# Late modulation rows from DMA transposes and VectorE product-sums, and half of the row statistics on ScalarE, in an adaLN + linear attention + SwiGLU block

## The chip, the cores and the metric

One NeuronCore of a Trainium2 chip runs the whole kernel in one launch. The metric is the device time in microseconds (us), the median of several runs. Below, PE is TensorE, DVE is VectorE, ACT is ScalarE, POOL is GpSimd, and SP is the engine that issues most of the DMAs (SPq and ACTq are the DMA-issuing parts of SP and ACT).

## What is computed

Everything is bf16, with S = 2048 rows, D = 1024, F = 3584 and 32 heads of width 32.

```python
x = A_x
mod = (silu(c) @ w_mod).reshape(1, 6, 1, D)        # w_mod is 1024 x 6144
sa, ca, ga, sb, cb, gb = mod[:, 0] ... mod[:, 5]    # six rows of D numbers
h = layernorm(x) * (1 + ca) + sa
q, k, v = split(h @ wqkv);  pq, pk = phi(q), phi(k) # phi(t) = (t+1 if t>0 else exp(t)) + 1e-6
o = (pq @ (pk^T v)) / (pq . sum(pk) + 1e-6)         # per head
x = x + ga * (o @ wo)
h = layernorm(x) * (1 + cb) + sb
out = x + gb * ((silu(h @ w_gate) * (h @ w_up)) @ w_down)
```

The rows `sa` and `ca` are needed at once; `ga`, `sb`, `cb`, `gb` are "late": each is silu(c), a vector of 1024, times a 1024 x 1024 slice of `w_mod`.

## The kernel before

The rows of x are cut into 16 tiles of 128 rows, and four tiles make a chunk of 512. Weights stay in a few large SBUF regions (M12, M3, M4, M5, M6, M7), of which views are used one after the other; `M4` holds the normalized, transposed and modulated activations of all four chunks.

**The order of work** is written out by hand. `add` appends a labelled step to `seq`; a label is (stage, chunk, number). `put` hangs further steps on a label, to be issued just after it. At the end a loop issues `seq` in order (lines 688 to 691). Every engine executes its own instructions in the order in which this loop issues them, and an instruction that waits holds up what stands behind it on its engine. The steps, in order: V,0 (eight groups); then for each chunk sc the stages KV,sc and, interleaved, Q,0 (only after chunk 0), K,sc+1 (eight groups) and V,sc+1 (eight groups); then Q,1 to Q,3 with the attention output; then GU,0 to GU,3 (28 steps of gate and up for each chunk); and D (down projection).

A **group** is eight matmuls of 128x512 into one PSUM bank. `nextbank` (line 237) hands out banks 0 to 4 in turn, so a group can begin when the group five before it has been taken out of its bank. For K and Q the bank is emptied by `phi_to` (line 242): one exp on ACT (L244), then two instructions on DVE (L245, L246). For V it is emptied by one copy on ACT (L267).

**Row statistics and normalization of a tile** (`ln`, line 223): DVE computes the statistics (`ln_stats`, L203 to L207), POOL computes the inverse deviation and shift (L209, L211) and the normalized tile (L218, 128x1024), and SP issues a DMA transpose into M4 (L227). Later `modulate` (L231, on DVE) applies 1+ca and sa. For chunk sc+1 these steps hang on K,sc,1 / 3 / 5 / 7 and V,sc,4 / 6 (lines 601 to 604).

**The late rows** come in blocks of 512 columns (`load_late`, 1 MB each, L299). Three ways lead from a block to the numbers: `late_vec` (L328) does `cb` on PE, 32 matmuls with one column each for a block; `late_sum` (L305, L307) does `ga`, `sb`, `gb` on DVE, eight instructions of 128x512 for a block that multiply by silu(c) per partition and add up in fp32, leaving a sum over partitions to be done; `late_split` (L312, L313) cuts this sum into a high and a low bf16 part, and PE sums over the partitions, with `late_cols` (L320, 8 matmuls with one column for a block) for `sb` and `late_bc` (L342, two 128x512 matmuls for a block, then a copy by ACT, L343) for `ga` and `gb`, which are wanted on all partitions. `ga` multiplies `wo` (L637) at K,3,2 to V,3,1 and `gb` multiplies `w_down` (L683) in GU,1, both on DVE.

Of the kernel before, what the change touches and what calls it, by code (L numbers as in the profile page):

```python
# [8 lines left out]
ACT = mybir.ActivationFunctionType  # L9
# [12 lines left out]
def kernel(  # L22
# [64 lines left out]
    def view(region, off, shape, dtype=BF16):  # L87
        n = 1
        for s_ in shape:
            n *= s_  # L90
        w = n * (2 if dtype == F32 else 1)
        ap = region[:, off:off + w]
        if dtype == F32:
            ap = ap.bitcast(F32)
        if len(shape) == 2:
            ap = ap.rearrange("p (a b) -> p a b", a=shape[0])
        elif len(shape) == 3:
            ap = ap.rearrange("p (a b c) -> p a b c", a=shape[0], b=shape[1])
        return ap
# [5 lines left out]
    wd_lo = view(M12, 14336, [14, D])  # L105
    wme = view(M3, 0, [DC, 2 * D])
    pqT = view(M3, 0, [NSC, HG, SCW])
    wml = [view(M3, 4096 * (1 + i), [DC, NB]) for i in range(3)]
    wd_hi = view(M3, 0, [14, D])
    pk = view(M5, 0, [STC, D])  # L110
    v_c = view(M5, 4096, [STC, HG, VW])
# [9 lines left out]
    accA = view(M5, 8256, [D], F32)  # L121
    hlA = [view(M5, 10304 + 1024 * i, [2, NB]) for i in range(2)]
    accG = view(M3, 12288, [D], F32)
    hlG = view(M3, 14336, [2, NB])
# [14 lines left out]
    def load_x(st):  # L139
        nc.sync.dma_start(out=xs[st % 6], in_=x2[st * P:(st + 1) * P, :])  # L140
# [43 lines left out]
    ones = const.tile([P, P], BF16, name="ones")  # L184
    nc.gpsimd.memset(ones[:], 1.0)
    scF = const.tile([P, DC], F32, name="scF")

    scT = const.tile([P, DC], BF16, name="scT")
    nc.scalar.activation(out=scT[:], in_=c_sb[:], func=ACT.Silu)
    nc.scalar.copy(out=scF[:], in_=scT[:])  # L190

    def warm(n):
        for _ in range(n):
# [5 lines left out]
    def ln_stats(st):  # L199
# [12 lines left out]
                                op0=ALU.mult, op1=ALU.mult)  # L212
        stat[st] = (rstd, nmr)

    def ln_xn(st, pool):
        rstd, nmr = stat.pop(st)
        if pool:
            nc.gpsimd.tensor_scalar(out=xns[st % 6], in0=xs[st % 6], scalar1=rstd[:], scalar2=nmr[:],  # L218
                                    op0=ALU.mult, op1=ALU.add)
# [81 lines left out]
    def late_sum(acc, kb, slot, js):  # L301
        dst = acc[:, kb * NB:(kb + 1) * NB]
        for j in js:
            if j == 0:
                nc.vector.tensor_scalar_mul(out=dst, in0=wml[slot][:, 0, :], scalar1=scF[:, 0:1])  # L305
            else:
                nc.vector.scalar_tensor_tensor(out=dst, in0=wml[slot][:, j, :], scalar=scF[:, j:j + 1], in1=dst,  # L307
                                         op0=ALU.mult, op1=ALU.add)

    def late_split(acc, kb, hl):  # L310
        src = acc[:, kb * NB:(kb + 1) * NB]
        nc.vector.tensor_copy(out=hl[:, 0, :], in_=src)  # L312
        nc.vector.tensor_tensor(out=hl[:, 1, :], in0=src, in1=hl[:, 0, :], op=ALU.subtract)  # L313

    def late_cols(q, kb, hl):
        o = 320 + 8 * q
        for ii in range(NB // P):
            col = o + kb * (NB // P) + ii
            for s_ in range(2):
                nc.tensor.matmul(bank[7][:, col:col + 1], lhsT=hl[:, s_, ii * P:(ii + 1) * P], rhs=ones[:, 0:1],  # L320
                                 start=False, stop=(s_ == 1), skip_group_check=True)

    def late_vec(q, kb, slot):
        o = 320 + 8 * q
        for ii in range(NB // P):
            col = o + kb * (NB // P) + ii
            for j in range(DC):
                nc.tensor.matmul(bank[7][:, col:col + 1], lhsT=wml[slot][:, j, ii * P:(ii + 1) * P],  # L328
                                 rhs=scT[:, j:j + 1], start=False, stop=(j == DC - 1), skip_group_check=True)

    def late_fin(q):
        mps = bank[7][:, 320 + 8 * q:328 + 8 * q]
        if q == SB:
            nc.vector.tensor_copy(out=sbT[:], in_=mps)
        else:
            nc.vector.tensor_copy(out=m1[:, q, :], in_=mps)
            nc.vector.tensor_scalar_add(out=cb1T[:], in0=m1[:, q, :], scalar1=1.0)

    def late_bc(kb, hl, dst):
        b = nextbank()  # L340
        for s_ in range(2):
            nc.tensor.matmul(b[:], lhsT=ones[:], rhs=hl[:, s_, :], start=(s_ == 0), stop=(s_ == 1))  # L342
        nc.scalar.copy(out=dst[:, kb * NB:(kb + 1) * NB], in_=b[:])  # L343


    def tr0(st):
# [101 lines left out]
    def put(label, *fns):  # L448
        after.setdefault(label, []).extend(fns)
# [159 lines left out]
    def sums(acc, kb, slot, labels):  # L609
        for i, lab in enumerate(labels):  # L610
            put(lab, lambda i=i: late_sum(acc, kb, slot, (2 * i, 2 * i + 1)))
# [4 lines left out]
    put(("V", 1, 7), lambda: late_fin(CB))  # L616
    sums(accA, 0, 2, [("V", 1, k) for k in range(4)])
    put(("V", 1, 3), lambda: late_split(accA, 0, hlA[0]), lambda: load_late(SB, 1, 2))
    put(("K", 2, 2), lambda: late_bc(0, hlA[0], ga_bc))
    put(("K", 2, 3), lambda: nc.sync.dma_start(out=wo, in_=wo_v))  # L620
    sums(accA, 1, 0, [("V", 2, k) for k in range(4)])
    put(("V", 2, 3), lambda: late_split(accA, 1, hlA[1]))
    put(("K", 3, 0), lambda: late_bc(1, hlA[1], ga_bc))
    for kb in range(2):
        sums(accA, kb, 1 + kb, [("V", 3, 4 * kb + k) for k in range(4)])
    put(("V", 3, 4), lambda: late_split(accA, 0, hlA[0]))
    put(("KV", 3, 0), lambda: late_split(accA, 1, hlA[1]))
    put(("Q", 1, 2), lambda: late_cols(SB, 0, hlA[0]), lambda: late_cols(SB, 1, hlA[1]), lambda: late_fin(SB))
    put(("GU", 0, 18), lambda: load_late(GB, 0, 0), lambda: load_late(GB, 1, 1))
    gb_at = [("GU", 0, f) for f in range(21, FC)] + [("GU", 1, f) for f in range(8)]  # L630
    for kb in range(2):
        sums(accG, kb, kb, gb_at[5 * kb:5 * kb + 4])
        put(gb_at[5 * kb + 3], lambda kb=kb: late_split(accG, kb, hlG))
        put(gb_at[5 * kb + 5], lambda kb=kb: late_bc(kb, hlG, gb_bc))
# [88 lines left out]
```

## Time and profile before

| | |
|---|---|
| time, median of 3 runs | 842.72 us (842.72 to 843.25) |
| the profiled execution: its time / its span | 842.25 us / 840.4 us |
| granted TensorE clock | 0.999 |
| busy PE / DVE / ACT / POOL | 833.5 / 356.5 / 145.1 / 79.9 us |
| DMA | 128.62 MB, 153 GB/s in the mean |
| late rows: loads of `w_mod` | 8 of 1 MB |
| DMA transposes issued by SP / by ACT | 12 / 32 |

The span runs from the first to the last instruction; the execution's own time is 1.85 us longer. The profile gives, for each engine, when each instruction ran and what ended the idle time ahead of it; the chain of waits is followed back from the last instruction, at each step to what released it. V,0 begins at about 31 us of the span, K,1,0 at 60.7 us, K,2,0 at 90.7, K,3,0 at 120.6, Q,1,0 at 150.4, GU,0 at 210, GU,1 at 346 us.

### The profile page before, as it was taken

The page shows a single profiled execution, that of the slowest core. Times are in us where ns is not written, and L with a number is a line of the kernel's source. Part 1 is how long each engine was busy: PE and PEld are TensorE (multiplying, and loading weights), DVE is VectorE, ACT ScalarE, POOL GpSimd, SP SyncE. Part 2 cuts the span into 40 slices and gives each one's busy share as a digit, 9 for nine tenths or more (in the row PEclk, how much of TensorE's full clock was granted, in tenths as well). Part 3 has the DMA queues.
Part 4 walks back from the last instruction along what each step waited for, and adds up shares of the span by engine and source line. Part 5 has one row for each costly group of instructions (what it writes and reads, how often), then busy time and mean ns, then how long its engine had stood idle before and what let it go on. Part 6 is the DMA issues. An engine that isn't in the chain of part 4 may idle for free.

```text
span 840.4 us, 10723 instructions
## 1 busy us (share of the span) xinstructions
PE 833.5 (99%) x4292; PEld 391.3 (47%) x4292; DVE 356.5 (42%) x668; ACT 145.1 (17%) x271; POOL 79.9 (10%) x143
## 2 busy tenths in 40 slices
PE   8999999999999999999999999999999999999998
PEld 4454444544444444444444444444444444444445
DVE  5768779988655656635341111111101211111111
ACT  4333333323211111111110001111000111100000
POOL 2124220022122323100000000000000000000000
PEclk9999999999999999999999999999999999999999
DMA  9985491056599899787874225555322555211210
GB/s 291 310 244 138 133 243 46 16 154 133 126 225 225 224 226 287 190 248 226 251 241 142 76 69 151 151 151 152 105 75 82 156 155 152 76 38 44 76 69 26
DMA packets 203905, 128.62 MB, mean 153 GB/s; under 512 B 50768, under 2 KB 190032, under 8 KB 203856
## 3 DMA queue, kind: packets, MB, share of 16 engines
q1 hardware_dynamic: 163008, 98.58, 41.1%
q10 hardware_dynamic: 38544, 20.98, 11.4%
q0 software_dynamic: 2304, 8.39, 2.6%
q8 instruction: 33, 0.54, 0.3%
q14 instruction: 16, 0.13, 0.1%
HBM read 103.81 MB, written 12.58 MB: 139 GB/s over the span
## 4 chain that ended last, share of the span: by engine, by line
PE 97%; SPq 1%; DMA 1%; issue 0%; DVE 0%
PE bank L553 23%; PE bank L534 23%; PE bank L528 23%; PE bank L272 7%; PE bank L485 7%; PE bank L264 7%; PE bank L249 6%; DMA M<-in_w_mod_dram 1%; PE bank L458 1%; PE bank L281 1%; SPq L148 1%; SPq L145 0%; PE bank L342 0%; SPq L140 0%; PE bank L328 0%; PE bank L364 0%
## 5 line engine op out<-in xcount | busy, mean ns | idle before, releaser
L534 PE MATMUL bank<-M,M 128*128 128x512 bf16 x896 | 211.7, 379 | 0.0
L528 PE MATMUL bank<-M,M 128*128 128x512 bf16 x896 | 211.6, 379 | 0.0
L536 DVE TENSOR_TENSOR M<-bank,e 128x512 bf16<-128x512 f32 x112 | 77.5, 692 | 248.5 <-PE bank L534 247.1
L553 PE MATMUL bank<-M,M 128*128 128x512 bf16 (+2 forms) x728 | 148.0, 363 | 0.0
L531 ACT ACTIVATE e<-bank 128x512 f32<-128x512 f32 x112 | 66.8, 597 | 436.3 <-PE bank L528 423.6
L553 PEld LDWEIGHTS <-M 128*128 128x128 bf16 x952 | 90.9, 98 | 103.0
L534 PEld LDWEIGHTS <-M 128*128 128x128 bf16 x896 | 87.7, 98 | 105.7
L528 PEld LDWEIGHTS <-M 128*128 128x128 bf16 x896 | 87.3, 98 | 103.9
L556 DVE TENSOR_TENSOR M<-bank,M 128x512 bf16<-128x512 f32 (+2 forms) x34 | 22.5, 661 | 169.9 <-PE bank L553 169.9
L249 PE MATMUL bank<-M,M 128*128 128x512 bf16 x256 | 57.9, 379 | 1.0 <-DVE M L231 0.6
L485 PE MATMUL bank<-M,M 128*128 128x512 bf16 x256 | 57.9, 379 | 0.0
L272 PE MATMUL bank<-M,M 128*128 128x512 bf16 x256 | 57.7, 379 | 0.0
L264 PE MATMUL bank<-M,M 128*128 128x512 bf16 x256 | 55.9, 379 | 0.0
L244 ACT ACTIVATE e<-bank 128x512 f32<-128x512 f32 x64 | 37.8, 598 | 100.5 <-PE bank L272 48.8
L553 PE MATMUL bank<-M 128*128 128x512 bf16 x224 | 51.0, 379 | 0.0
L246 DVE SCALAR_TENSOR_TENSOR M<-bank,e 128x512 bf16<-128x512 f32 x64 | 44.3, 692 | 3.9
L264 PEld LDWEIGHTS <-M 128*128 128x128 bf16 x256 | 25.0, 98 | 30.2
L485 PEld LDWEIGHTS <-M 128*128 128x128 bf16 x256 | 25.0, 98 | 29.7
L249 PEld LDWEIGHTS <-M 128*128 128x128 bf16 x256 | 24.2, 98 | 29.5 <-DVE M L231 2.1
L245 DVE TENSOR_SCALAR e<-e 128x512 f32<-128x512 f32 x64 | 27.7, 433 | 23.4 <-ACT e L244 23.4
L272 PEld LDWEIGHTS <-M 128*128 128x128 bf16 x256 | 24.5, 98 | 27.6
L487 DVE TENSOR_TENSOR M<-bank,M 128x512 f32<-128x512 f32 x32 | 22.0, 689 | 13.3 <-PE bank L485 13.1
(74 smaller groups left out, 362.4 us busy)
## 6 DMA issues: line engine op xcount, KB each, us to landing
M<-in_B_w_gate_dram SPq DMA_DIRECT2D x56, 512.0 KB, 3.9
M<-in_B_w_up_dram SPq DMA_DIRECT2D x56, 512.0 KB, 4.9
M<-in_w_mod_dram SPq DMA_DIRECT2D x8, 1024.0 KB, 8.7
x_scratch<-M POOLq DMA_DIRECT2D x16, 512.0 KB, 5.6
M<-x_scratch ACTq DMA_DIRECT2D x16, 512.0 KB, 3.4
M<-in_B_w_down_dram SPq DMA_DIRECT2D x6, 1024.0 KB, 7.9
M<-in_A_x_dram SPq DMA_DIRECT2D x16, 256.0 KB, 6.6
M<-in_w_mod_dram SPq DMA_DIRECT2D x8, 512.0 KB, 7.1
```

Source lines behind the costliest of these rows:

```text
L244: nc.scalar.activation(out=e[:], in_=acc, func=ACT.Exp)
L245: nc.vector.tensor_scalar(out=e[:], in0=e[:], scalar1=1.0, scalar2=PHI_EPS, op0=ALU.min, op1=ALU.add)
L246: nc.vector.scalar_tensor_tensor(out=dst, in0=acc, scalar=0.0, in1=e[:], op0=ALU.max, op1=ALU.add)
L249: nc.tensor.matmul(acc[:], lhsT=M4[:, sc_, cc, t * P:(t + 1) * P], rhs=wk[:, cc, h * NB:(h + 1) * NB], start=(cc == 0), stop=(cc == DC - 1))
L264: nc.tensor.matmul(acc[:], lhsT=M4[:, sc_, cc, t * P:(t + 1) * P], rhs=wv[:, cc, h * NB:(h + 1) * NB], start=(cc == 0), stop=(cc == DC - 1))
L272: nc.tensor.matmul(acc[:], lhsT=wq[:, cc, qc * P:(qc + 1) * P], rhs=M4[:, sc_, cc, :], start=(cc == 0), stop=(cc == DC - 1))
L485: nc.tensor.matmul(acc[:], lhsT=oTs[st % 3][:, cc, :], rhs=wo[:, cc, hs], start=(cc == 0), stop=(cc == DC - 1))
L528: nc.tensor.matmul(g_ps[:], lhsT=wg_blk[:, cc, fs], rhs=M4[:, sc_, cc, :], start=(cc == 0), stop=(cc == DC - 1))
L531: nc.scalar.activation(out=sg[:], in_=g_ps[:], func=ACT.Silu)
L534: nc.tensor.matmul(u_ps[:], lhsT=wu_blk[:, cc, fs], rhs=M4[:, sc_, cc, :], start=(cc == 0), stop=(cc == DC - 1))
L536: nc.vector.tensor_tensor(out=gus[sc_][:, f, :], in0=u_ps[:], in1=sg[:], op=ALU.mult)
L553: nc.tensor.matmul(y_ps[:, 0:w], lhsT=gus[sc_][:, f, t * P:(t + 1) * P], rhs=wd(f)[:, c0:c1], start=(f == 0), stop=(f == FC - 1))
```

## The change

- **Late rows.** For each of `ga`, `cb`, `sb`, `gb` eight DMA transposes read `w_mod` from HBM straight into a transposed view `rowT` (the output column lies on the partitions). One DVE instruction for each block of 128 columns (`tensor_tensor_reduce`, 128x1024) multiplies with silu(c), spread over all partitions in `sc_bc`, and sums to one number per partition in `colF`; its elementwise products go to a scratch tile `prod`. `late_vec`, `late_split`, `late_cols` and the ones-matmuls are gone. Where a row is wanted on all partitions (`sc_bc`, `ga_bc`, `gb_bc`), DVE spreads the column over a 128x1024 tile (`spread`), PE transposes it in eight 128x128 pieces, and ACT copies 128x1024 out.
- **Places.** One transpose hangs on each step of Q,0 (`ga`), V,1 (`cb`), V,2 (`sb`) and GU,0,18 to 25 (`gb`); one product-sum on each step of V,1, V,2, V,3 and GU,1,0 to 7. `cb` uses the region of `wo`, so the load of `wo` is issued after the last product-sum of `cb`, at V,2,7 (before: at K,2,3); the multiplication of `wo` by `ga` starts at K,3,4 (before: K,3,2), that of `w_down` by `gb` at GU,1,10 (before: GU,1,7).
- **Row statistics.** Tiles 9, 11, 13, 15 (the odd ones of chunks 2 and 3) get their statistics on ACT: a Copy and a Square of 128x1024, both with an accumulated row sum; POOL turns these into mean, variance, inverse deviation and shift. The `ln` steps move to K,sc,0 / 1 / 3 / 4 and the modulations to V,sc,2 / 3. The load of x tiles 12 to 15 moves from V,1,7 to K,1,7.

```diff
+    rowT = [view(M3, 4096, [DC, DC, P]), view(M6, 0, [DC, DC, P])]
+    prod = [view(M5, 8256, [D], F32), view(M3, 12288, [D], F32)]
...
-    gb_bc = const.tile([P, D], BF16, name="gb_bc")
+    gb_bc = ga_bc
...
+    def ln_stats_act(st):
+        x_sb = xs[st % 6]
+        sm = small.tile([P, 2], F32, name="sm")
+        nc.scalar.activation(out=xns[st % 6], in_=x_sb, func=ACT.Copy, accum_out=sm[:, 0:1])
+        nmean = small.tile([P, 1], F32, name="nmean")
+        nc.gpsimd.tensor_scalar_mul(out=nmean[:], in0=sm[:, 0:1], scalar1=-1.0 / D)
+        nc.scalar.activation(out=xns[st % 6], in_=x_sb, func=ACT.Square, bias=nmean[:], accum_out=sm[:, 1:2])
+        veps = small.tile([P, 1], F32, name="veps")
+        nc.gpsimd.tensor_scalar(out=veps[:], in0=sm[:, 1:2], scalar1=1.0 / D, scalar2=LN_EPS,
+                                op0=ALU.mult, op1=ALU.add)
+        rstd = small.tile([P, 1], F32, name="rstd")
+        nc.gpsimd.tensor_tensor(out=rstd[:], in0=veps[:], in1=neg_half[:], op=ALU.pow)
+        nmr = small.tile([P, 1], F32, name="nmr")
+        nc.gpsimd.tensor_tensor(out=nmr[:], in0=nmean[:], in1=rstd[:], op=ALU.mult)
+        stat[st] = (rstd, nmr)
...
     def ln(st):
-        ln_stats(st)
+        if st >= 2 * STC and st % 2:
+            ln_stats_act(st)
+        else:
+            ln_stats(st)
         ln_xn(st, True)
         sc_, t = divmod(st, STC)
         nc.sync.dma_start_transpose(out=M4[:, sc_, :, t * P:(t + 1) * P], in_=xns[st % 6])
...
-    def load_late(q, kb, slot):
-        k0 = q * D + kb * NB
-        nc.sync.dma_start(out=wml[slot], in_=wm_v[:, :, k0:k0 + NB])
...
+    def load_late(q, i, js):
         for j in js:
+            nc.sync.dma_start_transpose(out=rowT[i][:, j], in_=wm_v[:, j, q * D:(q + 1) * D])
+
+    def late_sum(q, i, pr, bs):
+        for b in bs:
+            nc.vector.tensor_tensor_reduce(out=prod[pr].rearrange("p (j k) -> p j k", j=DC), in0=rowT[i][:, :, b, :],
+                                           in1=sc_bc[:].rearrange("p (j k) -> p j k", j=DC), scale=1.0, scalar=0.0,
+                                           op0=ALU.mult, op1=ALU.add, accum_out=colF[:, q, b:b + 1])
+
+    def late_fin(q):
+        if q == SB:
+            nc.vector.tensor_copy(out=sbT[:], in_=colF[:, q, :])
+        else:
+            nc.vector.tensor_copy(out=m1[:, q, :], in_=colF[:, q, :])
+            if q == CB:
+                nc.vector.tensor_scalar_add(out=cb1T[:], in0=m1[:, q, :], scalar1=1.0)
             else:
+                spread(nc.vector, m1[:, q, :])
+
+    def spread(eng, col):
+        eng.tensor_copy(out=rep[:], in_=col.unsqueeze(2).to_broadcast([P, DC, P]))
+
+    def late_bc(dst):
+        tp = nextbank()[:].bitcast(BF16).rearrange("p (c s) -> p c s", c=DC)
+        for cc in range(DC):
+            nc.tensor.transpose(tp[:, cc, :], rep[:, cc, :], ident[:])
+        nc.scalar.copy(out=dst[:].rearrange("p (c s) -> p c s", c=DC), in_=tp)
...
     for cc in range(6, 8):
         modulate(0, cc, saT, ca1T)
+    spread(nc.vector, scT[:])
     for cc in range(6):
...
     for sc in (2, 3):
-        put_ln(sc, [("K", sc - 1, 1), ("K", sc - 1, 3), ("K", sc - 1, 5), ("K", sc - 1, 7),
-                    ("V", sc - 1, 4), ("V", sc - 1, 6)])
+        put_ln(sc, [("K", sc - 1, 0), ("K", sc - 1, 1), ("K", sc - 1, 3), ("K", sc - 1, 4),
+                    ("V", sc - 1, 2), ("V", sc - 1, 3)])
     put(("V", 0, 7), lambda: [load_x(st) for st in range(8, 12)])
-    put(("V", 1, 7), lambda: [load_x(st) for st in range(12, 16)])
...
-    put(("V", 0, 6), lambda: load_late(CB, 0, 0), lambda: load_late(CB, 1, 1), lambda: load_late(GA, 0, 2))
-    put(("K", 1, 2), lambda: late_vec(CB, 0, 0), lambda: load_late(GA, 1, 0))
-    put(("K", 1, 6), lambda: late_vec(CB, 1, 1), lambda: load_late(SB, 0, 1))
...
-    put(("K", 2, 3), lambda: nc.sync.dma_start(out=wo, in_=wo_v))
-    sums(accA, 1, 0, [("V", 2, k) for k in range(4)])
...
-    put(("Q", 1, 2), lambda: late_cols(SB, 0, hlA[0]), lambda: late_cols(SB, 1, hlA[1]), lambda: late_fin(SB))
-    put(("GU", 0, 18), lambda: load_late(GB, 0, 0), lambda: load_late(GB, 1, 1))
...
+    put(("K", 1, 7), lambda: [load_x(st) for st in range(12, 16)])
+
+
+    put(("V", 0, 5), lambda: late_bc(sc_bc))
+
+    def put_late(q, i, loads, sums, pr=0):
+        for k in range(DC):
+            put(loads[k], lambda k=k: load_late(q, i, (k,)))
+            put(sums[k], lambda k=k: late_sum(q, i, pr, (k,)))
+        put(sums[-1], lambda: late_fin(q))
+
+    put_late(GA, 0, [("Q", 0, k) for k in range(8)], [("V", 1, k) for k in range(8)])
+    put(("K", 2, 3), lambda: late_bc(ga_bc))
+    put_late(CB, 1, [("V", 1, k) for k in range(8)], [("V", 2, k) for k in range(8)])
+    put(("V", 2, 7), lambda: nc.sync.dma_start(out=wo, in_=wo_v))
+    put_late(SB, 0, [("V", 2, k) for k in range(8)], [("V", 3, k) for k in range(8)])
+    put_late(GB, 0, [("GU", 0, 18 + k) for k in range(8)], [("GU", 1, k) for k in range(8)], 1)
+    put(("GU", 1, 8), lambda: late_bc(gb_bc))
     for cc in range(DC):
-        put(("K", 3, 2 + cc) if cc < 6 else ("V", 3, cc - 6),
-            lambda cc=cc: nc.vector.tensor_tensor(out=wo[:, cc, :], in0=wo[:, cc, :], in1=ga_bc[:], op=ALU.mult))
+        put(("K", 3, 4 + cc) if cc < 4 else ("V", 3, cc - 4), lambda cc=cc: nc.vector.tensor_tensor(out=wo[:, cc, :], in0=wo[:, cc, :], in1=ga_bc[:],
+                                                               op=ALU.mult))
...
     for i in range(8):
         for k, f in enumerate(wd_f[i]):
-            put(("GU", 1, max(3 * i + 4, 7 + i) + k // 2) if i < 7 else ("GU", 1, FC - 2 + k),
+            put(("GU", 1, (10, 12, 14, 16, 17, 20, 23, 26)[i] + k // 2),
                 lambda f=f: nc.vector.tensor_tensor(out=wd(f), in0=wd(f), in1=gb_bc[:], op=ALU.mult))
```

More of the change, by code (lines that the diff above doesn't have):

```diff
@@ L107 @@
     pqT = view(M3, 0, [NSC, HG, SCW])
-    wml = [view(M3, 4096 * (1 + i), [DC, NB]) for i in range(3)]
     wd_hi = view(M3, 0, [14, D])
@@ L120 @@
     obs = [view(M6, 4096 + 1024 * i, [D]) for i in range(2)]
[L121 to L124, printed above, removed]
+    rowT = [view(M3, 4096, [DC, DC, P]), view(M6, 0, [DC, DC, P])]
+    prod = [view(M5, 8256, [D], F32), view(M3, 12288, [D], F32)]
     xs = [view(M7, 1024 * i, [D]) for i in range(6)]
@@ L181 @@
     ga_bc = const.tile([P, D], BF16, name="ga_bc")
-    gb_bc = const.tile([P, D], BF16, name="gb_bc")
+    gb_bc = ga_bc
     KVZ = const.tile([P, HG, KVW], BF16, name="KVZ")
-    ones = const.tile([P, P], BF16, name="ones")
-    nc.gpsimd.memset(ones[:], 1.0)
-    scF = const.tile([P, DC], F32, name="scF")
+    rep = const.tile([P, DC, P], BF16, name="rep")
+    sc_bc = const.tile([P, D], BF16, name="sc_bc")
+    colF = const.tile([P, 6, DC], F32, name="colF")
     scT = const.tile([P, DC], BF16, name="scT")
     nc.scalar.activation(out=scT[:], in_=c_sb[:], func=ACT.Silu)
-    nc.scalar.copy(out=scF[:], in_=scT[:])
     def warm(n):
@@ L295 @@
     GA, SB, CB, GB = 2, 3, 4, 5
-    def load_late(q, kb, slot):
-        k0 = q * D + kb * NB
-        nc.sync.dma_start(out=wml[slot], in_=wm_v[:, :, k0:k0 + NB])
-    def late_sum(acc, kb, slot, js):
-        dst = acc[:, kb * NB:(kb + 1) * NB]
-        for j in js:
-            if j == 0:
-                nc.vector.tensor_scalar_mul(out=dst, in0=wml[slot][:, 0, :], scalar1=scF[:, 0:1])
-            else:
-                nc.vector.scalar_tensor_tensor(out=dst, in0=wml[slot][:, j, :], scalar=scF[:, j:j + 1], in1=dst,
-                                         op0=ALU.mult, op1=ALU.add)
@@ L310, in late_split @@
[L310 to L343, printed above, removed]
+    def load_late(q, i, js):
+        for j in js:
+            nc.sync.dma_start_transpose(out=rowT[i][:, j], in_=wm_v[:, j, q * D:(q + 1) * D])
[4 more added lines that the diff above has]
+                                           op0=ALU.mult, op1=ALU.add, accum_out=colF[:, q, b:b + 1])
@@ L602 @@
     for sc in (2, 3):
-        put_ln(sc, [("K", sc - 1, 1), ("K", sc - 1, 3), ("K", sc - 1, 5), ("K", sc - 1, 7),
-                    ("V", sc - 1, 4), ("V", sc - 1, 6)])
+        put_ln(sc, [("K", sc - 1, 0), ("K", sc - 1, 1), ("K", sc - 1, 3), ("K", sc - 1, 4),
+                    ("V", sc - 1, 2), ("V", sc - 1, 3)])
     put(("V", 0, 7), lambda: [load_x(st) for st in range(8, 12)])
-    put(("V", 1, 7), lambda: [load_x(st) for st in range(12, 16)])
-    def sums(acc, kb, slot, labels):
-        for i, lab in enumerate(labels):
-            put(lab, lambda i=i: late_sum(acc, kb, slot, (2 * i, 2 * i + 1)))
@@ L613 @@
-    put(("V", 0, 6), lambda: load_late(CB, 0, 0), lambda: load_late(CB, 1, 1), lambda: load_late(GA, 0, 2))
-    put(("K", 1, 2), lambda: late_vec(CB, 0, 0), lambda: load_late(GA, 1, 0))
-    put(("K", 1, 6), lambda: late_vec(CB, 1, 1), lambda: load_late(SB, 0, 1))
[L616 to L619, printed above, removed]
@@ L620 @@
-    put(("K", 2, 3), lambda: nc.sync.dma_start(out=wo, in_=wo_v))
-    sums(accA, 1, 0, [("V", 2, k) for k in range(4)])
[L622 to L627, printed above, removed]
-    put(("Q", 1, 2), lambda: late_cols(SB, 0, hlA[0]), lambda: late_cols(SB, 1, hlA[1]), lambda: late_fin(SB))
@@ L629 @@
-    put(("GU", 0, 18), lambda: load_late(GB, 0, 0), lambda: load_late(GB, 1, 1))
[L630 to L634, printed above, removed]
+    put(("K", 1, 7), lambda: [load_x(st) for st in range(12, 16)])
+    put(("V", 0, 5), lambda: late_bc(sc_bc))
```

## The prediction

> **What bounds the kernel now.** I read the page first: busy times and the chain of waits.
>
> ```profile
> PE 833.5 (99%) x4292; PEld 391.3 (47%) x4292; DVE 356.5 (42%) x668; ACT 145.1 (17%) x271; POOL 79.9 (10%) x143
> ...
> PE 97%; SPq 1%; DMA 1%; issue 0%; DVE 0%
> ```
>
> PE is the bound: from 31 us on the chain is matmuls alone. PE work removed comes off the end one for one, and whatever makes PE wait comes on top. Next, PE's timeline, for what the removed matmuls cost (columns: start, us, instruction):
>
> ```profile
> 65.72 0.94 PE L328 MATMUL bank<-scT,M 128*128 128x1 bf16 x32
> 66.53 7.07 PE L249 MATMUL bank<-M,M 128*128 128x512 bf16 x32
> ...
> 96.77 0.59 PE L342 MATMUL bank<-M,ones 128*128 128x512 bf16 x2
> 97.20 8.80 PE L249 MATMUL bank<-M,M 128*128 128x512 bf16 x40
> ```
>
> Ends overlap, so I count start to start: 0.81 us for 32 one-column matmuls, 0.43 for a pair of 128x512. The chain gives 13.81 us for the 64 matmuls of a V stage, so a group takes 1.727. Last, the timelines of DVE, POOL and ACT around tile 8 in K,1:
>
> ```profile
> 65.97 1.27 DVE L203 BATCH_NORM_STATS2 stats<-M 128x6 f32<-128x512 bf16 x2
> ...
> 67.59 0.15 DVE L207 TENSOR_SCALAR veps<-mv 128x1 f32<-128x1 f32 x1
> ```
>
> ```profile
> 67.89 0.59 POOL L209 TENSOR_TENSOR rstd<-veps,neg_half 128x1 f32<-128x1 f32 x1 [19.93 <-DVE veps L207]
> 68.58 0.27 POOL L211 TENSOR_SCALAR nmr<-mv,rstd 128x1 f32<-128x1 f32 x1
> 68.95 1.46 POOL L218 TENSOR_SCALAR M<-M,rstd,nmr 128x1024 bf16<-128x1024 bf16 x1
> ```
>
> ```profile
> 68.45 0.60 ACT L244 ACTIVATE e<-bank 128x512 f32<-128x512 f32 x1 [1.93 <-PE bank L249]
> 70.18 0.60 ACT L244 ACTIVATE e<-bank 128x512 f32<-128x512 f32 x1 [1.13 <-PE bank L249]
> ```
>
> From the start of DVE's statistics (65.97) to the end of POOL's normalization (70.41) a tile takes 4.44 us. ACT meanwhile waits for PE alone: each exp starts as its group ends. That promptness is what the change touches.
>
> [...] L683, 1024 in bf16, takes 683 ns, L556, 512 in fp32, 692. The product-sum writes fp32, so it runs at the slow rate. [...] the built order has a 128x1 entry behind each product-sum. [...] L221 takes 1.24. [...] The trace has transposes out of SBUF only.
>
> **PE work.** Removed: two `late_vec` blocks 2 x 0.81, four ones-pairs 4 x 0.43, `late_cols` 0.41 (156.51 to 156.92): 3.75 us. Added: three times eight 128x128 transposes, at the 0.46 that L349's eight take (7.69 to 8.15): 1.38. All on the path, so -2.37 us; the rows are exact, I allow 0.2.
>
> **Unit costs of the new operations.** Product-sum: L556 goes from 425 ns (256 columns) to 692 (512), 1.04 ns per column, so 1.22 us for 1024, plus about 0.15 (as L207) for the accumulator: 1.4 with its wait; bounds 1.25 and 1.6. `spread` to 128x1024: 0.7 (L357's copy) to 1.3 (slow rate), I take 1.0. [...] POOL's small steps 0.25 to 0.6 each (L492, L209). DMA transpose: SP spends 1.25 us to issue one and SBUF ones land in 3.2[...]. Bytes stay 8 MB. None of these can gain below its own price, as nothing of PE depends on them being slow.
>
> **The moved statistics, the part that decides.** Copy and Square sit on ACT between two exps, and Square waits for `nmean` from POOL. POOL works in order, and `nmean` of tile 9 stands behind the normalization of tile 8, which waits for DVE. So the exps queued behind Square wait for DVE and POOL, and PE, five banks deep, waits for them: a group's bank is due four groups after the group's end. Clock t from the start of K,1,0:
>
> - K,1,0 ends 1.73, exp to 2.36, DVE phi to 3.53. Statistics of tile 8 start, POOL ends it 3.53 + 4.44 = 7.97. `nmean` 8.35, Square(9) to 9.7. Exp of K,1,2, ready at 5.2, ends 10.3; phi of K,1,2 to 11.4, of K,1,3 to 12.5.
> - Statistics of tile 10 start 12.5, POOL ends 16.95, `nmean` 17.3, Square(11) to 18.65, exp of K,1,5 to 19.25, phi to 20.35. V,1,2 wants that bank at 10 x 1.727 = 17.27: PE waits **3.1 us**.
> - V,1: DVE finishes K,1,7 at 22.5. Eight product-sums 11.2, eight modulations 2.6 (87.73 to 90.32), copy and `spread` 1.2: to 37.5. Tile 11's transpose lands at 24.7, DVE comes to it at 25.3. The modulations end near 29.3, before PE needs them.
> - K,2,0 starts at 20.35 + 6 x 1.727 + 0.9 (KV) = 31.6; its phi could start at 33.95 but runs 37.5 to 38.6. The same chain: POOL 43.0, Square(13) 44.7, phi of K,2,2 to 46.4. K,2,6 wants the bank at 43.3 (the `ga` broadcast takes a turn and 0.46): PE waits **3.1**. Phi of K,2,3 to 47.5, tile 14 to 51.95, Square(15) to 53.65, phi of K,2,5 to 55.35; V,2,2 wants it at 53.3: **2.0**.
>
> Sum 8.2 us. With product-sum and `spread` at their ends the second wait moves by -1.5 to +1.9, with Square 0.1 off each wait moves 0.1 to 0.2: 5.5 to 10.5. What DVE saves (8 x 0.69 statistics, two fewer small steps per tile) is spent on waiting for ACT.
>
> **The other moves, costed at nothing, and their cover.** `wo` waits for the last `cb` product-sum, 71.4 on this clock, and lands 10.2 us later as before: 82.1. DVE stands at it after K,3,4; phi of K,3,5 then ends 83.8, and V,3,2 wants its bank at 84.8. Cover 1.0 us, gone if the eight `sb` transposes (seven ahead of `wo` on SP, from 57.8) take over 2.1 us each. SP: `ga` transposes start near 51 us of the span, when 3 MB of late loads are no longer in the way, and have until 84; `cb` has 20 us; x tiles 12 to 15 land by t = 31 and are needed at 38.6. First `spread`: DVE idles 27.2 to 28.9. ACT's three copies of 0.99 and the removed `scF` and `ones`: ACT idles 1.13 us between groups; the start hangs on loads. V,3: DVE does 11.2 + 2.4 us where it did 14, so Q,1 starts as before. GU: 3.45 us a step against 0.69 + 1.4 on DVE; the `gb` chain (sum, copy, `spread`) takes about 3.35 after GU,1,7 and PE asks at 3.45. GB's transposes delay ACT's own by some us at GU,0,18 to 26, where ACT idles 2.9 to 6.3 us at a time. The `w_down` products come later but have until D,0.
>
> **Sum.** -2.37 + 8.2 = +5.8 us. On the profiled execution 842.25 + 5.8 = 848.1; its own time lies 0.47 below the median of the runs, so 848.5 against 842.72, slower by 0.7%.
>
> **Rivals.**
> - *The detour fits* (faster): if POOL and ACT go through the chain more quickly, no exp comes too late and only the PE saving is left, 842.72 - 2.37 = 840.4. For: ACT is busy 17%, POOL 10%. Against: the wait is made of serial steps with measured lengths. It decides where each of the two POOL passes of a chunk is 1.6 us shorter than I have it. Chance 0.15.
> - *Half of it*: waits of 1 to 4 us in all, because DVE gets to the statistics sooner or the later waits swallow each other; 841.4 to 844.4, say 843. Chance 0.10.
> - *HBM transposes are slow* (slower still): at 3 us each the seven ahead of `wo` end 57.8 + 21 = 78.8 instead of before 71.4; 7.4 less the 1.0 of cover puts 6.4 on PE: 855; at 4 us 862. For: 256-byte pieces out of rows 96 KB apart, never traced here. Against: SBUF ones keep to 1.25. Chance 0.15.
> - The forecast, 844.5 to 852: chance 0.60.
>
> That the late rows don't leave PE is no case: the built order has none of the old late matmuls.
>
> **The numbers.** About 0.2% (1.7 us) is what a measurement here can tell from no change: faster 0.15 (first rival), same 0.10 (second), slower 0.75. Range 840.0 to 853.0: it takes in the fast rival and the forecast with its bounds, and leaves out most of the slow one and a little below, under 0.2. The forecast's own range is 845 to 851.5.
>
> **What would show it.** In the timeline: ACT idle ahead of Square, released by POOL, some 3 us for tiles 9 to 15; PE idle before V,1,2, K,2,6 and V,2,2, released by DVE, about 8 us in all; product-sums near 1.4 us with their accumulator; [...] no DVE wait for `wo` that reaches PE. Wrong if PE shows no gap in K,1 to V,2 (then the first rival), or if its gaps are released by DMA (then the third).

## The result, and the profile after

| | before | after |
|---|---|---|
| time, median | 842.76 us (842.72 to 843.25, 4 runs) | 858.35 us (855.89 to 858.69, 4 runs) |
| profiled execution: time / span | 842.25 / 840.4 us | 855.89 / 854.1 us |
| granted TensorE clock there | 0.999 | 0.998 |

The changed kernel takes 1.0177 times as long (95% interval 1.0158 to 1.0197), 15.6 us more; the range reached to 853. Its profiled execution is the quickest of its four and lies 13.6 us above that of before. The line numbers of this section are those of the changed kernel. PE's share and the chain of waits, from the page of after:

```profile
PE 828.7 (97%) x4148; PEld 389.8 (46%) x4228; DVE 351.4 (41%) x661; ACT 152.5 (18%) x285; POOL 78.6 (9%) x150
...
PE 85%; DVE 5%; DMA 4%; issue 2%; SPq 1%; POOL 1%; ACTq 1%; ACT 1%; DVEq 0%; POOLq 0%
```

PE's share of the chain has fallen from 97% to 85%, and DVE and DMA have come in: PE now waits for others. (The page has 4148 matmuls to 4228 weight loads, where that of before has 4292 of each: some matmul records are missing. A missing record can show as a gap, as at 362.95 below, where one and six matmuls of a group of eight stand with 0.22 us between them, so the sums below are made from the starts of stages and groups.) Where the loss arises is read by setting the same label side by side in the two timelines of PE:

| stage begins, us of the span | before | after | difference |
|---|---|---|---|
| V,0 | 31.10 | 31.27 | +0.17 |
| K,1,0 | 60.54 | 61.16 | +0.62 |
| KV,2 (after V,1,0 to 7 and K,1) | 89.77 | 92.09 | +2.32 |
| KV,3 (after K,2 and V,2) | 119.65 | 126.10 | +6.45 |
| GU,0 | 210.25 | 216.26 | +6.01 |
| last matmuls of D | 785.55 | 798.89 | +13.34 |

Two stretches lose time: K,1 to V,2, and GU (with its neighbour GU,1). In the first stretch the timeline of PE shows these waits (start, us, instruction, idle before it):

```profile
77.08 1.89 PE L279 MATMUL bank<-M,M 128*128 128x512 bf16 x8 [0.43 <-DVE M L261]
81.57 10.68 PE L279 MATMUL bank<-M,M 128*128 128x512 bf16 x47 [2.60 <-DVE M L261]
...
106.38 3.77 PE L264 MATMUL bank<-M,M 128*128 128x512 bf16 x15 [1.51 <-DVE M L261]
...
115.58 10.68 PE L279 MATMUL bank<-M,M 128*128 128x512 bf16 x47 [1.97 <-DVE M L261]
```

L261 is the second DVE step of phi: a bank comes free too late, at V,1, at K,2,6 and in V,2. The timelines of ACT and POOL around tiles 8 to 11 tell why (L214 is Copy with the sum, L217 Square; L205 to L230 normalize the tile of VectorE):

```profile
65.31 1.05 ACT L214 ACTIVATE M<-M 128x1024 bf16<-128x1024 bf16 x1
66.25 0.19 ACT L214 ACTIVATION_READ_ACCUMULATOR M<-M 128x1 f32 x1
69.27 1.15 ACT L217 ACTIVATE M<-M,nmean 128x1024 bf16<-128x1024 bf16 x1 [2.82 <-POOL nmean L216]
...
70.42 1.55 ACT L259 ACTIVATE e<-bank 128x512 f32<-128x512 f32 x3
...
78.54 1.15 ACT L217 ACTIVATE M<-M,nmean 128x1024 bf16<-128x1024 bf16 x1 [5.54 <-POOL nmean L216]
```

```profile
66.78 0.59 POOL L205 TENSOR_TENSOR rstd<-veps,neg_half 128x1 f32<-128x1 f32 x1 [18.69 <-DVE veps L203]
...
67.84 1.19 POOL L230 TENSOR_SCALAR M<-M,rstd,nmr 128x1024 bf16<-128x1024 bf16 x1
69.00 0.23 POOL L216 TENSOR_SCALAR nmean<-sm 128x1 f32<-128x1 f32 x1
```

ACT has the sum of tile 9 at 66.44, but POOL is at the normalization of tile 8 until 69.03 and only then scales the mean (L216). Square (L217) stands in ACT's order and waits 2.82 us; behind it three exps have piled up, which run back to back at 70.42. Before, each exp began as its group ended.

In GU,0 the waits are of another kind. PE's timeline of after:

```profile
327.52 1.89 PE L482 MATMUL bank<-M,M 128*128 128x512 bf16 x8
330.56 1.89 PE L482 MATMUL bank<-M,M 128*128 128x512 bf16 x8 [1.15 <-ACT e L528]
...
356.45 1.89 PE L525 MATMUL bank<-M,M 128*128 128x512 bf16 x8
362.95 0.58 PE L531 MATMUL bank<-M,M 128*128 128x512 bf16 x1 [4.61 <-ACT e L528]
363.76 2.75 PE L531 MATMUL bank<-M,M 128*128 128x512 bf16 x6 [0.22 <-issue]
366.32 1.92 PE L525 MATMUL bank<-M,M 128*128 128x512 bf16 x8
```

PE is held by a late silu (L528). ACT's timeline of the same stretch, with its DMA issues (ACTq; L501 is its transpose of a normalized tile into M4):

```profile
327.86 1.95 ACTq L501 DMA_TRANSPOSE M<-M  x1
329.91 0.60 ACT L528 ACTIVATE e<-bank 128x512 f32<-128x512 f32 x1 [13.62 <-PE bank L482]
...
360.95 1.25 ACTq L501 DMA_TRANSPOSE M<-M  x1
362.30 1.57 ACT L528 ACTIVATE e<-bank 128x512 f32<-128x512 f32 x3 [12.38 <-issue]
```

ACT stands still 13.62 and 12.38 us ahead of its silus, where its longest regular wait there is 6.3. The releaser in brackets is no help: three silus in a row at 362.30 mean that their matmuls had long been done. What ended the two waits is in the chain, asked for these windows alone (start, us, what; SP's L314 reads `gb`'s part of `w_mod` transposed, ACT's L470 is another transpose out of SBUF):

```profile
316.80 8.63 DMA M<-in_w_mod_dram
...
325.58 1.25 ACTq L470
...
347.49 4.46 DMA M<-M
352.00 1.23 SPq L314
...
354.54 6.35 DMA M<-in_w_mod_dram
...
360.95 1.25 ACTq L501
```

Ahead of the first late silu one transpose of SP is under way from 316.80 for 8.63 us, and ACT issues L470 at 325.58, 0.15 after its landing. Ahead of the second there are two landings: ACT's transpose issued at 347.49 takes 4.46, and SP issues one at 352.00, 0.05 after it; SP's next one takes 6.35 from 354.54, and ACT issues its own at 360.95, 0.06 after that. The silu stands behind that issue, and PE behind the silu. SP's list of waits has the same order from its side (us in total, times, longest):

```profile
SPq L314 <- DMA M<-M: 27.8, 4, 8.0
```

The sum of the trace is complete. First stretch: the start 0.17, waits of 3.32 (K,1 to V,1: 2.32 - 0.62, plus 1.62 of `late_vec` that is gone) and of 4.1 (K,2 to V,2), against 1.97 of PE work saved by then, and some 0.4 in Q: +6.0. Second stretch, from start to start of the groups, where eight matmuls take 1.73: 1.31 at 330.56 and 4.77 at 362.95, and 1.64 because the eight matmuls from 362.95 took 3.37 us: 7.72, less 0.40 of `gb`'s ones-matmuls: +7.32 of the 7.33 found. The last 0.4 of the 13.7 us between the two spans arise after the last row of the table and were not followed.

### The profile page after: what moved, and what is told of

The parts are those of the page before. It is cut to its first block, busy times and chain, and to the rows that moved or that the text cites. A ratio compares the mean times of both kernels' runs of the same rounds, so it can differ in the third digit from the quotient of the medians.

```text
span 854.1 us, 10559 instructions
## 1 busy us (share of the span) xinstructions
PE 828.7 (97%) x4148; PEld 389.8 (46%) x4228; DVE 351.4 (41%) x661; ACT 152.5 (18%) x285; POOL 78.6 (9%) x150
## 4 chain that ended last, share of the span: by engine, by line
PE 85%; DVE 5%; DMA 4%; issue 2%; SPq 1%; POOL 1%; ACTq 1%; ACT 1%; DVEq 0%; POOLq 0%
PE bank L550 23%; PE bank L531 21%; PE bank L525 21%; PE bank L482 5%; PE bank L287 5%; PE bank L279 4%; PE bank L264 4%; DMA M<-in_w_mod_dram 3%; DVE M L318 1%; DVE M L261 1%; PE bank L455 1%; DVE e L260 1%; PE bank L296 1%; ACTq L501 1%; SPq L145 1%
## 5 line engine op out<-in xcount | busy, mean ns | idle before, releaser
L528 ACT ACTIVATE e<-bank 128x512 f32<-128x512 f32 x112 | 66.3, 598 | 446.0 <-PE bank L525 372.0
L261 DVE SCALAR_TENSOR_TENSOR M<-bank,e 128x512 bf16<-128x512 f32 x64 | 44.2, 691 | 3.9
L260 DVE TENSOR_SCALAR e<-e 128x512 f32<-128x512 f32 x64 | 30.7, 480 | 29.6 <-ACT e L259 29.6
L318 DVE CUSTOM_DVE_ANT_0 M<-M,sc_bc 128x1024 f32<-128x1024 bf16 x32 | 39.0, 1219 | 0.5
```

What stands on the lines that cost most here:

```text
L260: nc.vector.tensor_scalar(out=e[:], in0=e[:], scalar1=1.0, scalar2=PHI_EPS, op0=ALU.min, op1=ALU.add)
L261: nc.vector.scalar_tensor_tensor(out=dst, in0=acc, scalar=0.0, in1=e[:], op0=ALU.max, op1=ALU.add)
L318: nc.vector.tensor_tensor_reduce(out=prod[pr].rearrange("p (j k) -> p j k", j=DC), in0=rowT[i][:, :, b, :], in1=sc_bc[:].rearrange("p (j k ...
L528: nc.scalar.activation(out=sg[:], in_=g_ps[:], func=ACT.Silu)
```

## The experiments

The theory after the result: two waits that have nothing to do with each other. (A) A ScalarE tile's mean stands on POOL behind the normalization of the VectorE tile before it; the exps behind Square come late. (B) The two queues that issue DMA transposes wait for each other, and ACT's silus stand behind the waiting issues. Rivals: VectorE is overloaded by 32 product-sums; reading `w_mod` transposed takes too much of the DMA; the statistics alone make all of it. The shared median of before is 842.53 us for the first four, 842.44 for the next four and 842.48 for the last two.

| run | edit | median, us | ratio to before (95%) |
|---|---|---|---|
| e1_swap | ScalarE tile first | 851.04 | 1.0097 (1.0077 to 1.0118) |
| e2_gb_later | `gb` transposes later | 848.89 | 1.0068 (1.0051 to 1.0086) |
| e3_gb_plain | `gb` loaded untransposed | 848.86 | 1.0072 (1.0057 to 1.0087) |
| e4_dve_stats | all statistics on VectorE | 849.77 | 1.0088 (1.007 to 1.0105) |
| e5_swap_gb_later | e1 and e2 | 842.06 | 0.9994 (0.9987 to 1.0002) |
| e6_dve_gb_later | e4 and e2 | 841.84 | 0.999 (0.9981 to 1.0) |
| e7_stats_only | before, with the statistics moved | 850.55 | 1.0093 (1.0077 to 1.0108) |
| e8_gb_on_act | `gb` transposes issued by ScalarE | 849.01 | 1.0077 (1.0063 to 1.009) |
| e9_swap_gb_after | e1, `gb` after all of ScalarE's transposes | 840.88 | 0.998 (0.9971 to 0.9988) |
| e10_stats_only_swap | e7, ScalarE tile first | 847.9 | 1.0062 (1.005 to 1.0075) |

### Wait A: the order of two tiles on POOL

**e1_swap.**

```diff
-        put_ln(sc, [("K", sc - 1, 0), ("K", sc - 1, 1), ("K", sc - 1, 3), ("K", sc - 1, 4),
+        put_ln(sc, [("K", sc - 1, 1), ("K", sc - 1, 0), ("K", sc - 1, 4), ("K", sc - 1, 3),
```

> The changed kernel with one thing moved: in chunks 2 and 3 the tile whose statistics ACT takes is issued ahead of its DVE partner (tile 9 after K,1,0 and tile 8 after K,1,1; 11 ahead of 10, 13 ahead of 12, 15 ahead of 14). All work is the same; only nmean of an ACT tile no longer stands behind its partner's normalization on POOL. Theory (the PE waits in K,1 to V,2 come from Square waiting for nmean in POOL's order): the ACT waits ahead of Square, 2.8 to 5.5 us now, shrink to under 3 us, PE's four waits (0.4, 2.6, 1.5, 2.0) go, and the time falls by about 7.5 us, to some 851 us (profiled 848). Rival (DVE is overloaded by the product-sums): DVE has the same work, PE keeps its waits, and the time stays within 2 us of the changed kernel's 858. The later loss in GU,0 stays in both.

Measured 851.04, 7.3 less than the changed kernel. Its waits (engine, line, releaser: us in total, times, longest) of PE and ACT:

```profile
PE bank L531 <- ACT e L528: 5.5, 2, 5.0
...
ACT M L217 <- POOL nmean L216: 5.1, 4, 2.7
```

Square waited 17.1 us in all in the changed kernel (longest 5.5) and waits 5.1 now; PE has no gap left in K,1 to V,2. Only the order of two tiles is different, so the wait is made by that order. The gaps in GU,0 stay, as the theory of two separate waits has it.

**e4_dve_stats.**

```diff
-        if st >= 2 * STC and st % 2:
+        if False:
```

> The changed kernel with the statistics of all tiles on DVE, at the places of the changed kernel; nothing of the late rows is touched. Theory (the detour over ACT and POOL is the cost): ACT never waits for POOL, PE's waits in K,1 to V,2 go although DVE has 6.9 us more work in chunks 2 and 3, time down by about 7.5 us to some 851 (profiled 848). Rival (DVE's load is what delays PE): DVE gets 3.4 us more in each K stage, the PE waits grow by 3 us or more, and the time goes up to some 861. The later loss in GU,0 stays in both.

Measured 849.77, no gap in K,1 to V,2, gaps of 1.2, 0.9 and 4.8 us in GU,0. VectorE carries the product-sums and all statistics, so an overloaded VectorE falls as the cause of these gaps.

**e7_stats_only.** The kernel before, with the new `ln_stats_act`, the new labels of `ln` and `modulate`, and the load of x tiles 12 to 15 at K,1,7:

```diff
+        if st >= 2 * STC and st % 2:
+            ln_stats_act(st)
+        else:
+            ln_stats(st)
...
+        put_ln(sc, [("K", sc - 1, 0), ("K", sc - 1, 1), ("K", sc - 1, 3), ("K", sc - 1, 4),
+                    ("V", sc - 1, 2), ("V", sc - 1, 3)])
```

> The kernel before with the moved statistics alone: tiles 9, 11, 13, 15 on ScalarE, the earlier places, x tiles 12 to 15 loaded at K,1,7; the late rows stay as they were before. Theory: the wait is made by the statistics themselves, a VectorE tile's normalization on POOL ahead of the ScalarE tile's mean, so 6 to 8 us of waits come also without the product-sums: about 849 us (847 to 851), gaps of PE at V,1 and in K,2 to V,2. Rival (the product-sums and spreads on VectorE push the statistics back and make the waits): at most the one wait of K,1 to V,1 stays, 843 to 846 us.

Measured 850.55, inside the theory's range, but the trace says that only part of it is wait A. Its stages stand against those of before by +2.42 at K,1,0, +4.11 at KV,2, +6.09 at KV,3 and +7.83 at Q,1. So the statistics alone make waits of 1.69 and 1.98, 3.7 us; the 2.4 were lost at the start, and 1.7 in K,3, and that the time fell inside the range is luck. Most of the loss at the start is clock: after a wait of 1.25 us for `w_mod`, 18 matmuls from 21.74 took 5.93 us at a granted clock down to 0.50, where in e1 they took 4.24 after a wait of 1.22. In the changed kernel wait A is 7.4: the difference in K,1 is 3.32 - 1.69 = 1.63, which is what `late_vec` took (1.62). There PE's own work had covered part of the wait, so taking it off PE gained nothing in that stage. The rest, about 2.1 us in K,2, fits the product-sums and `spread` ahead of phi on VectorE, as the rival has it; this share follows from the difference and was not tried by itself.

**e10_stats_only_swap.** The same with the two tiles of each pair swapped.

> The kernel before with the moved statistics alone, and in each pair the ScalarE tile ahead of its VectorE partner. Theory: the wait of 5.4 us that the unswapped order makes between K,1 and K,3 goes; PE work is that of the kernel before, so 842.4 us (842 to 843.5). The 2.4 us by which V,0 began later in the profile of the unswapped kernel is chance at the start and not due to the statistics. Rival (it belongs to the moved statistics): 844.5 to 845.5 us, with V,0 beginning near 33.5 us of the span.

Measured 847.9: this expectation was wrong. V,0 begins at 31.43 us with the same statistics moved, so the lag at the start does not belong to them (whether the other runs of e7, within 0.8 us of the profiled one, had it too is not known), and wait A has shrunk (one gap of 0.46). But K,3 still loses 4.3 us. The waits of e10 on VectorE, its transposes on SP (L246 the transposes, L639 the load of `wo`), and PE's granted clock by stretches (us, busy PE, PEld, DVE, ACT, POOL, clock, DMA share, GB/s):

```profile
DVE M L250 <- DMA M<-M: 4.9, 1, 4.9
```

```profile
108.51 0.39 SPq L639 DMA_DIRECT2D M<-in_A_wo_dram  x1
110.08 3.78 SPq L246 DMA_TRANSPOSE M<-M  x1
```

```profile
124.00:126.00 2.00, 0.48 (x3) 0.12 (x3) 1.90 (x5) 0.60 (x1) 0.00 (x0) 0.88 1.20 291
126.00:128.00 2.00, 1.89 (x11) 1.13 (x12) 1.68 (x3) 0.59 (x1) 0.00 (x0) 0.50 1.20 290
128.00:130.00 2.00, 2.00 (x16) 1.41 (x14) 0.00 (x0) 0.00 (x0) 0.00 (x0) 0.77 1.13 271
```

The last tile's transpose stands behind the 2 MB load of `wo` and lands 9.7 us after its issue (the median is 3.1). Before, the modulations stood at V,2,4 and 6; at V,2,2 VectorE waits 4.9 us for it, PE then has gaps of 0.58 and 1.52, and right after them the granted clock is 0.50. So this is a third wait, of a modulation that was moved ahead of its data. In the changed kernel, where the load of `wo` went to V,2,7, K,3 loses nothing. The e7 run contains it too (its 1.7 us in K,3); that the two are the same was read from the traces, not tried.

### Wait B: two queues of transposes

**e2_gb_later.** The `gb` transposes to GU,0,25 to 27 and GU,1,0 to 4, with the steps that follow from them moved back:

```diff
-    put_late(GB, 0, [("GU", 0, 18 + k) for k in range(8)], [("GU", 1, k) for k in range(8)], 1)
-    put(("GU", 1, 8), lambda: late_bc(gb_bc))
+    put_late(GB, 0, [("GU", 0, 25 + k) if k < 3 else ("GU", 1, k - 3) for k in range(8)],
+             [("GU", 1, 6 + k) for k in range(8)], 1)
+    put(("GU", 1, 14), lambda: late_bc(gb_bc))
...
-            put(("GU", 1, (10, 12, 14, 16, 17, 20, 23, 26)[i] + k // 2),
+            put(("GU", 1, 15 + f * 13 // 28),
```

> The changed kernel with the eight gb transposes issued by SP after GU,0,25 to GU,1,4 in place of GU,0,18 to 25, that is, after the last DMA transpose that ACT issues; product-sums at GU,1,6 to 13, broadcast at GU,1,14, products of w_down from GU,1,15. Theory (transposes of SP and of ACT wait for each other, ACT stands in such a wait and the silus behind it come late): ACT's idle times of 8 to 14 us in GU,0 go back to some 6, PE's waits of 1.2 and 4.6 us and the slow matmuls after them go, time down by about 7.7 us to some 850.5 (profiled 848). Rival (transposes out of HBM are slow and take the DMA engines): the same bytes move beside the same weights, so a wait of some us comes back in GU,1, with the product-sums or the weights late, and at most 2 us are won.

Measured 848.89, 9.5 less than the changed kernel, and no gap of PE in GU. Of those of wait A the 2.60 and the 1.98 stay; the one in K,2 is gone, because PE came to K,2 1.5 us later: after the gap of 2.60 its clock fell (see the last section).

**e3_gb_plain.**

```diff
+            if q == GB:
+                nc.sync.dma_start(out=rowT[i][:, j], in_=wm_v[:, j, q * D:(q + 1) * D].rearrange("p (b k) -> p b k", b=DC))
+            else:
+                nc.sync.dma_start_transpose(out=rowT[i][:, j], in_=wm_v[:, j, q * D:(q + 1) * D])
```

> The changed kernel with the eight gb loads at their places but as plain copies of the same bytes into the same view, not transposed; the gb numbers, and with them the second half of the output, are therefore not the reference's. Theory (waits between the transposes of two queues): plain copies wait for none and none waits for them; GU,0 has no PE wait and the time falls by about 7.7 us to some 850.5 (profiled 848). Rival (2 MB more traffic at this place[...]): the same bytes in the same eight DMAs stay, so ACT still stands and at least 4 of the 7.7 us remain. The waits in K,1 to V,2 stay in both.

This kernel leaves out the transposition, so its `gb`, and with it its output, is not the reference's; only its time is used. Measured 848.86. The same bytes at the same steps, not transposed, and the gaps of GU are gone. All that PE waits for after the start in this run is wait A:

```profile
PE bank L279 <- DVE M L261: 4.8, 3, 2.6
PE bank L264 <- DVE M L261: 1.5, 1, 1.5
```

**e8_gb_on_act.**

```diff
-            nc.sync.dma_start_transpose(out=rowT[i][:, j], in_=wm_v[:, j, q * D:(q + 1) * D])
+            (nc.scalar if q == GB else nc.sync).dma_start_transpose(out=rowT[i][:, j], in_=wm_v[:, j, q * D:(q + 1) * D])
```

> The changed kernel with the eight transposes for gb at the same places, but issued by ScalarE instead of SP, so that all transposes of GU,0 stand in one queue. Theory (the cost in GU,0 is the waiting of the two transposing queues for each other): the gaps of 1.2 and 4.6 us shrink, though each issue now takes 1.25 us of ScalarE's own time, which is idle 2.9 to 6.3 us in each step there: 849 to 852 us. Rival (the cost is that eight more transposes are under way in these steps, whoever issues them): 857 to 860 us, gaps as before or larger.

Measured 849.01, the lower end of the theory. All transposes are there, at the old steps, and GU has no gap of PE. ACT's timeline shows the two kinds in one queue:

```profile
346.91 0.60 ACT L528 ACTIVATE e<-bank 128x512 f32<-128x512 f32 x1 [2.86 <-PE bank L525]
346.91 1.94 ACTq L314 DMA_TRANSPOSE M<-in_w_mod_dram  x1
348.95 3.38 ACTq L501 DMA_TRANSPOSE M<-M  x1
352.43 0.60 ACT L528 ACTIVATE e<-bank 128x512 f32<-128x512 f32 x1 [4.93 <-PE bank L531]
```

The longest hold-up of a silu by issues is about 2 us beyond its 2.86, where it was 12.38 in all with two queues. With e3 this settles B: not the bytes and not the number of transposes cost the time, but the waiting of one queue for the other.

### Both edits

**e5_swap_gb_later** (e1 and e2) and **e6_dve_gb_later** (e4 and e2).

> Both edits in one: in chunks 2 and 3 the tile whose statistics are on ScalarE goes ahead of its VectorE partner, and the transposes for gb stand after the last transposes that ScalarE issues in GU,0. Theory: the two waits are separate and add up, so both vanish and the PE saving of the change is left: 842.5 - 2.4 = 840.2 us, with 840 to 842 allowed for; no gap of PE over 0.5 us in K,1 to V,2 or in GU,0. Rival (removing one wait uncovers another one, for example of SP or of VectorE in GU,1, where gb now arrives seven steps later): 843 us or more, with a gap of PE in GU,1 or at the start of D.

> All row statistics on VectorE, and the transposes for gb after the last transposes that ScalarE issues in GU,0: what is left of the change is the late rows and the earlier places of the statistics. Theory: the PE saving alone, 840.2 us, with 840 to 842 allowed for. If moving half of the statistics to ScalarE is worth something once nothing waits for it, this run is slower than the one with both halves and the swapped order; the theory expects no difference between them over 0.5 us, as VectorE has slack in these stages. Rival: VectorE is overloaded by 16 product-sums and all statistics, gaps of PE released by VectorE in V,1 to V,2, 843 us or more.

Measured 842.06, just above what the theory allows, and 841.84, just inside, with single runs from 840.0 to 847.1. The two waits add up: e1 and e2 by themselves took 7.3 and 9.5 us off the changed kernel, both together 16.3. e5 and e6 differ by 0.2 us, less than the spread of either: no worth of statistics on ScalarE can be seen here. In e6 one gap of 1.62 is left in GU,0, and the timelines show where it is from; PE's gap first, then SP's transpose, then ACT's:

```profile
350.95 1.89 PE L531 MATMUL bank<-M,M 128*128 128x512 bf16 x8 [1.62 <-ACT e L528]
```

```profile
337.83 3.23 SPq L314 DMA_TRANSPOSE M<-in_w_mod_dram  x1
```

```profile
348.95 1.25 ACTq L501 DMA_TRANSPOSE M<-M  x1
350.30 1.58 ACT L528 ACTIVATE e<-bank 128x512 f32<-128x512 f32 x3 [10.70 <-PE bank L525]
```

One transpose of SP was still issued ahead of ACT's last one: it took 11.05 us to land from 337.83, and ACT's was issued 0.07 after that. Hence:

**e9_swap_gb_after.**

```diff
+    put_late(GB, 0, [("GU", 1, k) for k in range(8)], [("GU", 1, 8 + k) for k in range(8)], 1)
+    put(("GU", 1, 16), lambda: late_bc(gb_bc))
...
+            put(("GU", 1, 17 + f * 11 // 28),
```

> The swapped order of the statistics, and all eight transposes for gb at GU,1,0 to 7, after the last of ScalarE's own transposes (in the two kernels with both edits the first one, at GU,0,25, still stood ahead of ScalarE's last one, which then waited 11 us for it, and PE up to 1.6 us). Theory: with no transpose of SP between two of ScalarE's, PE has no gap left in GU and only the PE saving shows: 840.2 us, with 839.5 to 841.5 allowed for, and a narrower spread of the runs than the 840.0 to 844.8 of those two. Rival (the rest above 840.2 there came from the start of the program or from the clock): 841.5 to 842.5 us and the same spread. Work that comes too late in GU,1 (gb now at step 16, the products of w_down up to step 27) would show as a gap at D,0.

Measured 840.88, eleven of twelve runs between 840.52 and 841.23: quicker than both kernels, 1.6 us under before. The rival, that the rest came from elsewhere, falls: most of the spread went with the wait. Its trace has no gap of PE in GU and none in K,1 to V,2, and the end of D lies 1.75 us ahead of before (783.80 against 785.55).

## Why the prediction was wrong, step by step

- **What bounds the kernel.** Right for before, and "whatever makes PE wait comes on top" is what happened.
- **PE work, -2.37 us.** Right in size: e9 keeps it and gains 1.6, its trace 1.75, where 2.37 less the 0.45 below is 1.9. The transposes of a column set the next matmuls back by 0.45 (41.52 to 41.96 in e9), as priced; about 0.45 are lost to a later L455 in Q, at 168.62. But in K,1 the removed 1.62 only lengthened a wait.
- **Unit costs.** Those taken from the trace of before are inside their bounds or at them: product-sum 1.22 and its accumulator, a second instruction, 0.08, 1.27 start to start (1.4 taken); `spread` 0.69 (1.0). For Copy and Square with a sum and for transposes out of HBM that trace had no figure; the 1.35 us that the chain of the prediction gives Square was the author's estimate. Copy and Square take 1.05 and 1.15 with 0.19 each for the sum; transposes out of HBM land in 4.5 us in the median, 4.7 those of ACT out of SBUF, and eight of one row take 11.9 us or 1.49 each.
- **The moved statistics, 8.2 us of waits.** Right in mechanism, place and nearly in size: 3.32 where 3.1 stood, 4.1 where 3.1 and 2.0 stood; together 7.4. POOL's normalization took 1.19 instead of 1.46, and the product-sums were shorter. The bounds do not come out of their terms: 8.2 less 1.5 and three times 0.2 is 6.1 and not 5.5, and the forecast stands there once as 844.5 to 852 and once as 845 to 851.5. The miss does not hang on either.
- **"The other moves, costed at nothing".** Here the prediction failed, in one sentence: "GB's transposes delay ACT's own by some us at GU,0,18 to 26, where ACT idles 2.9 to 6.3 us at a time". The delay was not some us but up to 13.62 us of idle ACT: in the chain ACT's transposes at 325.58 and 360.95 are issued when one of SP's has landed, and SP's at 352.00 when one of ACT's has; without a second queue (e8) or without the transposition (e3) the gaps of PE in GU are gone. Compared with ACT's cover (6.3 and then five banks) the delay was too much: 7.7 us on PE. The trace of before could not show it, since there SP's last transposes are issued from 109.26 to 116.53 and ACT's first at 163.52. Given such an order, an estimate of its size follows from the landings before, 3.2 us for SP's and 4.7 for ACT's: two or three in turn on the way to one silu make 6 to 14 us. The 12.38 came about so, with landings of 4.46 and 6.35; behind the 13.62 stands one landing of 8.63, and why that one took so long is not shown.
- The rest of that paragraph held. VectorE waits 1.4 us for `wo` and PE doesn't feel it; the `gb` chain in GU,1 and V,3 cause no gap.
- **Sum.** 842.25 - 2.37 + 7.4 + 7.7 = 855.0, and the profiled execution took 855.89. The other three runs of the changed kernel took 2.2 to 2.8 us more, with a mean granted clock of 0.992 to 0.994 instead of 0.998. More time at a granted clock of 0.50 after a gap would look like this. There is no trace of them, but that of e2 shows it after the same gap of 2.60 us that left the clock alone in the changed kernel (see the last section), so this is the likely cause and not a shown one.
- **Rivals.** The detour didn't fit. Transposes out of HBM took 1.49 us each in a row, where the case that gave 855 to 862 had 3 to 4, so it was wrong though its time came out. That the issues of one queue could wait for the landings of another was among none of the cases, and so the range ended too low.

## What to carry to other kernels

When an operation is moved to a stage where another queue issues the same kind, look whether the two queues wait for each other: here SP's DMA transposes among ACT's had both issuing engines wait for landings, ACT's silus for up to 13.62 us, and all that stood behind the issue in that engine's order paid for it. The same transposes in one queue (e8) or in separate stages (e9) cost PE no gap. When a detour over a second and third engine puts a wait into an in-order engine, place the step that everybody waits for ahead of the long neighbour; here the exchange of two tiles was worth 7.3 us. And work taken off the bounding engine counts only in a stage where it does not merely come sooner to the next wait, as with the 1.62 us of `late_vec` in K,1.

## What the runs showed of the hardware

- PE's granted clock fell to 0.50 after some gaps. In the changed kernel, by stretches around the gap of 4.61 us (columns as above):

```profile
363.00:364.00 1.00, 0.78 (x2) 0.35 (x3) 1.00 (x2) 0.88 (x2) 0.00 (x0) 0.50 0.47 85
364.00:365.00 1.00, 1.00 (x3) 0.29 (x2) 1.00 (x4) 0.00 (x0) 0.00 (x0) 0.50 0.00 0
365.00:366.00 1.00, 1.00 (x4) 0.40 (x3) 1.00 (x4) 0.00 (x0) 0.00 (x0) 0.50 0.39 91
366.00:367.00 1.00, 1.00 (x6) 0.36 (x5) 1.00 (x4) 0.00 (x0) 0.00 (x0) 0.82 1.03 196
```

  Matmuls take 0.43 instead of 0.216 us for about 3 us, so this gap cost 1.64 us beyond its length. How long the gap is does not decide it alone. After the gap of 2.60 us at 81.57 the clock of the changed kernel stayed at 1.00, and the next 48 matmuls took 10.68 us. In e2, whose steps are the same up to there, it fell after a gap of the same length, and they took 12.21:

```profile
81.52 12.21 PE L279 MATMUL bank<-M,M 128*128 128x512 bf16 x48 [2.60 <-DVE M L261]
```

```profile
83.00:84.00 1.00, 1.00 (x4) 0.36 (x3) 0.90 (x3) 0.00 (x0) 0.00 (x0) 0.50 0.52 105
```

  In e2 it fell after the 1.98 in V,2 too (the next 48 matmuls took 12.21 us), in e8 after the 2.60 (12.01) and not after the 1.98 (10.68), and in e10 after 0.58 and 1.52 in a row (0.50 from 126 to 128 us). So gaps of the same length, 2.60 and 1.98 us, were followed by the half clock in some executions and not in others; what else decides it the runs do not show.
- Such a fall cost nothing where PE would have waited soon after anyway: in e8, as in the changed kernel, 64.94 us pass from K,1,0 to the start of KV,3, although the 48 matmuls after the 2.60 took 12.01 us and not 10.68; the gap ahead of K,2,6 shrank from 1.51 to 0.18.
- The first step of phi on VectorE (L260, 0.43 us) takes 1.18 and 1.17 us at 72.17 and 81.44 of the changed kernel, where it runs beside POOL's normalization of a tile (71.87 and 81.14).
